# Forgetting attention and a two-layer MLP on one core: more of the first layer by seven products

## The chip, the core and the metric

The kernel runs on one core of one Trainium2 chip. The metric is the device time of one execution in microseconds (us); lower is better. A core has a matrix engine (TensorE, PE in the profile, with its weight loads as PEld), a vector engine (VectorE, DVE), a scalar engine for activations and copies (ScalarE, ACT), a general engine (GpSimd, POOL), and SyncE (SP), which here only issues DMAs. SBUF is the on-chip memory with 128 partitions; PSUM takes the results of PE.

## The reference, cut to what matters

```python
# attention: B=8, H=8, S=576, D=64, float32 in and out
scores = scale * q @ k.T                       # scale = 1/8
cum    = cumsum(log(clip(f, 1e-4, 1)), -1)     # f: [B, H, S]
scores = where(causal, -1e9, scores + cum[..., :, None] - cum[..., None, :])
attn   = exp(scores - max(scores)); attn = attn / (sum(attn) + 1e-9)
x      = (attn @ v).transpose(0, 2, 1, 3).reshape(4608, 512)
# MLP: w_in [512, 2048], w_out [2048, 512]
g      = gelu_tanh(x @ w_in)
out    = g @ w_out                             # [4608, 512] float32
```

## The kernel before

**Tiling.** The 64 heads are worked through in 16 quads of four (quad i = 0..15, batch i // 2). The MLP goes over the 4608 tokens in nine chunks of 512 (c = 0..8). Attention writes its output transposed into `xT`, 128 partitions by 4 blocks of features by 4608 tokens, in bf16. The MLP of a chunk starts when the quads that cover its tokens are done. A *stage* below is one chunk: its first layer, then its second layer mixed with the attention of quads that later chunks need.

**Order.** Nothing is scheduled by a planner. Each engine works through its instructions in the order in which they are written, and that order is written by hand as tables of short words: `SETUP`, `FRONT` (attention of the first quads, chunks 0 and 1) and `TABLES[2]` to `TABLES[8]`. `run` and `play` look up each word and issue its instructions. In a table, `q2` means quad 2c + 2, and numbers behind dots are arguments. What may overlap is set by semaphores between engines and by the number of buffers per pool: in PSUM two of `psS` (scores, and first-layer results), one of `psO` (attention products, and one first-layer block when asked for), two of `psM` (second layer and parts of the units); in SBUF four of `snap` and four of `ostage`.

**Words of the attention.** `LK`, `LQ` load keys and queries (issued on POOL's queue), `TK`, `TQ` transpose them (DVE, 1.24 us each), `S` computes scores (PE, L261) and their exponentials (ACT, L269), `M` masks with a select on POOL (L275), `m` masks by a product with a triangle on DVE (L304), `VW` or `vw` weights the values (POOL or DVE), `CL` copies a corner of them, `D` computes denominators (PE, then two transposes and a reciprocal on DVE, L348 to L352, `den`), `V` multiplies by the values on PE into `po` (L329) and then by the reciprocal on DVE into `xT` (L360), in two halves `V.i.0` and `V.i.1`. `LV` loads values from SP's queue. `Y` and `X` load the tables of gelu and of exp on ACT.

**Words of the first layer.** `P.pr` (`mlp_in`) computes 256 features of all 512 tokens: eight matmuls 128x512 (L374) and one gelu 128x1024 (L381); pr = 0..7. `P.pr.1` puts the result into `psO` instead of `psS`. `R.k` (`seven_in`) advances a *unit*: it replaces the two blocks pr = k and pr = k + 4 by Strassen's method with seven products instead of eight, on a 2 by 2 split of weights and tokens. It is a generator; each `R.k` in a table runs it to its next `yield`. One unit is 28 matmuls 128x256 (L422) in seven groups of four, into two banks of `psS` (pa, pb) and two of `psM` (pc, pd); on DVE one copy p1 (L435) and five additions that build p1, u2 and v4 in `snap` tiles (L437, L440, L442, L448, L452); four gelus 128x512 (L431). The unit needs sums of token blocks (`T`, four DVE operations at L395, kept in the columns of `xT` of the chunk before) and of weight blocks (`K.k.n`, n = 0..3, four DVE operations at L410). The first three sums of weights of unit k are kept in the columns of `xT` of chunk `HOMES[k]`, which are no longer needed; the fourth is made in place in `w_in_sb`.

**Words of the second layer.** `O`, `F` and `f` advance the second layer of a chunk by that many groups (`seven_products`, L510; also by seven products on a 2 by 2 split). It needs sums of the gelus, `G` (`gelu_sums`, DVE L489 to L495), copies two of its products out on ACT (L531) and adds on DVE into `o_st` (L535), which SP stores. `O.512` at the head of each table finishes the second layer of the chunk before; `F.10 S.q3.0 D.q2 ... f.22 ...` mixes the current one with attention.

Units before: chunk 3 has one (R.1), chunks 4 to 8 have two (R.1 and R.3), the others none. In table 7 the first layer is the line

```python
Y O.512 P.0.1 R.1 P.4.1 R.1 R.1 R.3 P.2.1 R.3 G.0.1.2 P.6 R.3 G.0.3.4 G.1.1.2 F.40 T
```

so a block `P` stands between two parts of a unit and gives DVE time to finish its additions.

Of the kernel before, what the change touches and what calls it, by code (L numbers as in the profile page):

```python
# [16 lines left out]
def kernel(  # L17
# [21 lines left out]
    N_DT = D_MODEL // 128  # L39
# [6 lines left out]
    CH = 512  # L46
# [31 lines left out]
        J.0.2 J.1.2 X LK.4 F.0.6 TK.3 B.3.256 S.2.0 LK.5 F.0.9 S.2.2 F.0.10 S.2.1 TQ.3 TQ.4 F.0.10 LV.2.0@LK.5 m.2.1 vw.2 TK.4 S.3.0 f.0.1 M.2.2  # L78
        CL.2 LQ.5 M.2.0 D.2 f.0.6 S.3.1 m.3.0 F.0.6 V.2.0 S.3.2 TK.5 LK.6 M.3.2 f.0.7 V.2.1 CL.3 S.4.1 m.3.1 LQ.6 F.0.6 TQ.5 H.4.2.1 D.3 H.4.0.1
        LQ.7 VW.4 H.4.0.0 V.3.1 v.3.0 f.0.3 H.4.2.0 CL.4 I.1.0 m.4.1 U.0 LV.2.1@LQ.5 I.1.4 TQ.6 m.4.2.3 I.1.1 I.1.5 U.1 LV.3.0@LQ.7 LV.3.1 m.4.2.2  # L80
        TK.6 G.0 M.4.0 LK.7 LQ.8 LK.8 I.1.2 I.1.3 U.3 I.1.6 I.1.7 G.1.1.2 U.2 X F.1.16 S.5.0 f.1.26 S.5.1 D.4 M.5.0 f.1.16 S.5.2 V.4.0 m.5.2.3
        f.1.10 VW.5 V.4.1 CL.5 m.5.2.2 S.6.0 f.1.10 M.5.1 D.5 f.1.7 S.6.1 V.5.1 f.1.12 V.5.0 vw.6 S.6.2 m.6.1 M.6.2.2 m.6.0 m.6.2.3 CL.6
    """

    HOMES = {1: 0, 3: 1}
    TABLES = {}
    TABLES[2] = """
        Y O.512 P.0 P.1 TK.q3 TQ.q3 LK.q5 LQ.q5 TK.q4 TQ.q4 LK.q6 LQ.q6 LV P.4 P.5 G.0 P.2 P.3 P.6 P.7 G.1.1.2 X F.10 S.q3.0 D.q2 M.q3.0 f.22 S.q3.1
        V.q2.0 K.1.0 K.1.1 M.q3.1 VW.q3 f.18 S.q3.2 V.q2.1 M.q3.2 K.3.0 K.3.1 CL.q3 f.16 S.q4.0 VW.q4 D.q3 M.q4.0 f.18 S.q4.1 V.q3.0 K.1.2 K.1.3 K.3.2
# [15 lines left out]
        M.q4.1 f.13 V.q3.1 T f.3 CL.q4 S.q4.2  # L105
    """
    TABLES[6] = """
        Y O.512 P.0.1 R.1 P.4.1 R.1 R.1 LK.q5 LQ.q5 M.q2.2 LV R.3 P.2.1 R.3 G.0.1.2 P.6 R.3 G.0.3.4 G.1.1.2 X F.10 S.q3.0 D.q2 M.q3.0 f.22 S.q3.1
        V.q2.0 M.q3.1 VW.q3 f.18 S.q3.2 V.q2.1 M.q3.2 CL.q3 f.20 D.q3 f.18 V.q3.0 v.q3.1 T f.14
    """  # L110
    TABLES[7] = """
        Y O.512 P.0.1 R.1 P.4.1 R.1 R.1 R.3 P.2.1 R.3 G.0.1.2 P.6 R.3 G.0.3.4 G.1.1.2 F.40 T
    """
    TABLES[8] = """
        O.512 P.0.1 R.1 P.4.1 R.1 R.1 R.3 P.2.1 R.3 G.0.1.2 P.6 R.3 G.0.3.4 G.1.1.2
    """

    singles = ctx.enter_context(tc.tile_pool(name="singles", bufs=1))
    ostage_pool = ctx.enter_context(tc.tile_pool(name="ostage", bufs=4))
    snap_pool = ctx.enter_context(tc.tile_pool(name="snap", bufs=4))  # L120
    den_pool = ctx.enter_context(tc.tile_pool(name="den", bufs=1))
    rb_pool = ctx.enter_context(tc.tile_pool(name="rb", bufs=2))
    psS = ctx.enter_context(tc.tile_pool(name="psS", bufs=2, space=bass.MemoryType.PSUM))
    psO = ctx.enter_context(tc.tile_pool(name="psO", bufs=1, space=bass.MemoryType.PSUM))
    psM = ctx.enter_context(tc.tile_pool(name="psM", bufs=2, space=bass.MemoryType.PSUM))

    def many(n, shape, dtype, name):
        return [singles.tile(shape, dtype, name=f"{name}{i}") for i in range(n)]

    ident_f32 = singles.tile([BH, BH], FP32, name="ident_f32")  # L130
    utri_f32 = singles.tile([128, 128], FP32, name="utri_f32")
    ones_f32 = singles.tile([128, 128], FP32, name="ones_f32")

    q_c = many(2, [128, S // 32, D], BF16, "q_c")
    k_c = many(2, [128, S // 32, D], BF16, "k_c")
# [227 lines left out]
    def mlp_in(c, prs, spare=0):  # L363
# [40 lines left out]

    def w_sums(k, eng, which):

        a11, a12, a21, a22, s1, s2, s4 = w_blocks(k)
        todo = ((s1, a21, a22), (s2, s1, a11), (s4, a12, s2), (a21, a11, a21))
        for n in which or range(4):
            (eng.tensor_sub if n else eng.tensor_add)(*todo[n])  # L410

    def seven_in(c, k):

        a11, a12, s3, a22, s1, s2, s4 = w_blocks(k)
        b11, b12, b21, b22, t1, t2, t3, t4 = x_blocks(c)
        pa, pb = (psS.tile([128, 2, 512], FP32, name="ps_ab", tag="s")[:, 0].rearrange("p (j n) -> p j n", j=2) for _ in range(2))
        pc, pd = (psM.tile([128, 2, HC], FP32, name="ps_cd", tag="m") for _ in range(2))

        def multiply(ps, w, x, first):
            for j in range(2):  # L420
                for dt in range(2):
                    nc.tensor.matmul(ps[:, j], w[:, dt, 128 * j:128 * j + 128], x[:, dt],  # L422
                                     start=(first and j == 0 and dt == 0), stop=(dt == 1),
                                     skip_group_check=True)
# [10 lines left out]
        nc.vector.tensor_copy(p1, pa)  # L435
        multiply(pb, s2, t2, True)
        nc.vector.tensor_add(u2, pb, p1)  # L437
        multiply(pc, s1, t1, True)
        v4 = part()
        nc.vector.tensor_add(v4, pc, u2)  # L440
        multiply(pd, s3, t3, True)
        nc.vector.tensor_add(v4, pd, v4)  # L442
# [12 lines left out]

# [209 lines left out]
    def load_values(b, half):  # L665
# [35 lines left out]
        "F": out_part,  # L701
        "f": lambda c, n: out_part(c, n, 1),
        "K": lambda k, *which: w_sums(k, nc.vector, which),
        "B": keep_busy,
        "X": load_exp,
        "Y": load_gelu,
# [81 lines left out]
```

## Time and profile before

| | us |
|---|---|
| median of three runs (lowest, highest) | 325.47 (325.46, 325.60) |
| the profiled execution | 325.69 |
| its span (first to last instruction) | 324.00 |
| PE busy, 5479 instructions | 312.9 (97%) |
| DVE busy, 381 instructions | 242.2 (75%) |
| ACT busy, 245 instructions | 202.8 (63%) |
| POOL busy, 150 instructions | 107.8 (33%) |
| first layer of chunk 2 (no unit) | 101.92 to 115.76: 13.84 |
| first layer of chunk 3 (one unit) | 136.39 to 149.81: 13.42 |
| first layer of chunk 7 (two units) | 269.48 to 282.64: 13.16 |

Times in rows of the profile are microseconds from the span's start unless they are called ns. A row of the timeline gives the start, the busy time, the engine, the line of the kernel, the operation, the output and input by the kernel's names, the shapes and types, and how many instructions in a run it joins. Matmuls are pipelined, so the busy time of a run of them is longer than the distance to the next; the pace is read from the starts. A bracket gives the idle time ahead of a row and who ended it. Some matmul records are missing (a row with x7 where eight were issued).

### The profile page before, as it was taken

What the parts mean: (1) busy time and instruction counts of PE and PEld (TensorE: products, weight loads), DVE (VectorE), ACT (ScalarE), POOL (GpSimd) and SP (SyncE); (2) the same over time, 40 slices, a digit from 0 to 9 for tenths busy, and PEclk for the clock granted to TensorE, in tenths of its full rate; (3) what the DMA queues carried; (4) which work ended last, traced back from release to release, by engine and by line L of the source; (5) the groups of instructions that cost most, each with busy time, mean ns of one, the idle gap of its engine ahead of it and who ended that gap; (6) DMA issues with size and microseconds to landing.
All of it is one profiled execution on the core that took longest, in us unless ns stands there. A gap on an engine that the chain in (4) does not pass through costs nothing.

```text
span 324.0 us, 12192 instructions
## 1 busy us (share of the span) xinstructions
PE 312.9 (97%) x5479; PEld 214.5 (66%) x5499; DVE 242.2 (75%) x381; ACT 202.8 (63%) x245; POOL 107.8 (33%) x150
## 2 busy tenths in 40 slices
PE   3999999999999999999999999999999999999995
PEld 1357854544776467766777687667866786687684
DVE  5676138895769748978996899789977967885772
ACT  4585586776767677577657785678666842722630
POOL 8987554340320217302662047303720140000000
PEclk9999999999999999999999999999999999999999
DMA  7999999779201951285129611981120102012003
GB/s 130 204 208 209 194 225 203 151 142 234 58 4 67 220 108 36 67 177 79 36 66 182 149 36 36 166 195 38 36 67 0 35 15 89 0 35 97 3 32 99
DMA packets 46485, 33.45 MB, mean 103 GB/s; under 512 B 29792, under 2 KB 40160, under 8 KB 46432
## 3 DMA queue, kind: packets, MB, share of 16 engines
q0 software_dynamic: 8624, 15.99, 28.4%
q1 hardware_dynamic: 37664, 16.60, 19.4%
q8 instruction: 43, 0.70, 1.0%
q14 instruction: 10, 0.08, 0.1%
q10 hardware_dynamic: 144, 0.07, 0.1%
HBM read 36.85 MB, written 9.44 MB: 143 GB/s over the span
## 4 chain that ended last, share of the span: by engine, by line
PE 94%; POOL 2%; issue 1%; ACT 1%; DVE 1%; POOLq 0%; DVEq 0%; ACTq 0%
PE ps_w L510 30%; PE ps_h L374 22%; PE ps_s L261 10%; PE po L329 9%; PE ps_cd L422 6%; PE ps_ab L422 5%; PE ps_h L464 4%; PE pso L580 4%; PE po_m L315 1%; PE idle_ps L240 1%; ACT pt L269 1%; POOL v_nat L169 1%; PE ps_o L329 0%; DVE pt L304 0%; POOL q_c L192 0%
## 5 line engine op out<-in xcount | busy, mean ns | idle before, releaser
L269 ACT ACTIVATE pt<-ps_s 128x1024 bf16<-128x1024 f32 (+2 forms) x100 | 93.7, 988 | 36.9 <-PE ps_s L261 32.5
L275 POOL TENSOR_SCALAR_AFFINE_SELECT pt<-pt 128x512 bf16<-128x512 bf16 (+3 forms) x65 | 39.0, 610 | 117.5 <-ACT pt L269 116.5
L374 PE MATMUL ps_h<-xT,w_in_sb 128*128 128x512 bf16 x320 | 75.7, 379 | 0.8
L381 ACT ACTIVATE gT<-ps_h 128x1024 bf16<-128x1024 f32 x42 | 42.9, 1021 | 40.5 <-PE ps_h L374 40.1
L374 PEld LDWEIGHTS <-w_in_sb 128*128 128x128 bf16 x336 | 32.8, 98 | 34.6 <-issue 0.4
L510 PEld LDWEIGHTS <-gT 128*32 128x32 bf16 (+1 forms) x1247 | 50.7, 97 | 5.7 <-issue 1.7
L510 PE MATMUL ps_w<-w_out_sb,gT 128*32 128x256 bf16 (+1 forms) x1050 | 46.9, 273 | 0.0
L510 PEld LDWEIGHTS <-gsum 128*32 128x32 bf16 (+1 forms) x1256 | 39.1, 97 | 1.4
L261 PE MATMUL ps_s<-qT,kT 32*128 32x64 bf16 (+5 forms) x896 | 36.6, 265 | 0.1
L510 PE MATMUL ps_w<-usum,gsum 128*32 128x256 bf16 (+1 forms) x832 | 30.6, 273 | 0.0
L215 POOL TENSOR_TENSOR vw<-v_nat,wT 128x1280 bf16<-128x1280 f32 (+1 forms) x13 | 30.5, 2346 | 0.1
L198 DVE STREAM_TRANSPOSE kT<-k_c 128x576 f32<-128x576 f32 x16 | 19.9, 1244 | 14.1 <-DMA k_c<-in_k_dram 14.1
L535 DVE TENSOR_TENSOR o_st<-ps_w,snap 128x512 f32<-128x512 f32 x31 | 21.3, 690 | 10.5 <-PE ps_w L510 8.7
L261 PEld LDWEIGHTS <-kT 32*128 32x128 bf16 x896 | 16.6, 93 | 17.2 <-issue 12.3
L360 DVE TENSOR_TENSOR xT<-po,rb 128x576 bf16<-128x576 f32 x26 | 19.5, 751 | 5.9 <-PE po L329 5.4
L329 PE MATMUL po<-pt,vw 128*32 128x64 bf16 (+4 forms) x624 | 22.5, 279 | 0.0
L329 PEld LDWEIGHTS <-vw 128*32 128x32 bf16 x672 | 14.2, 97 | 10.5 <-issue 3.7
L422 PEld LDWEIGHTS <-w_in_sb 128*128 128x128 bf16 x176 | 17.2, 98 | 5.1 <-issue 0.8
L198 DVE STREAM_TRANSPOSE qT<-q_c 128x576 f32<-128x576 f32 x16 | 19.9, 1244 | 0.9 <-PE ps_s L261 0.7
L431 ACT ACTIVATE gT<-snap 128x512 bf16<-128x512 f32 x33 | 18.8, 623 | 0.7
L489 DVE TENSOR_TENSOR gsum<-gT 128x1024 bf16<-128x1024 bf16 x16 | 11.0, 685 | 11.1 <-ACT gT L381 11.1
L510 PE MATMUL ps_w<-usum,gT 128*128 128x256 bf16 (+1 forms) x197 | 16.9, 273 | 0.0
(100 smaller groups left out, 420.4 us busy)
## 6 DMA issues: line engine op xcount, KB each, us to landing
out_dram<-o_st SPq DMA_DIRECT2D x35, 256.0 KB, 2.3
k_c<-in_k_dram POOLq DMA_DIRECT2D x16, 288.0 KB, 5.5
q_c<-in_q_dram POOLq DMA_DIRECT2D x16, 288.0 KB, 6.9
v_nat<-in_v_dram SPq DMA_DIRECT2D x16, 256.0 KB, 6.1
v_nat<-in_v_dram SPq DMA_DIRECT2D x20, 128.0 KB, 4.9
w_in_sb<-in_moe_w_in_dram POOLq DMA_DIRECT2D x4, 512.0 KB, 10.0
w_out_sb<-in_moe_w_out_dram POOLq DMA_DIRECT2D x4, 512.0 KB, 8.8
v_nat<-in_v_dram POOLq DMA_DIRECT2D x9, 128.0 KB, 6.8
```

What stands on the lines that cost most here:

```text
L198: nc.vector.transpose(out=dst.rearrange("p s c -> p (s c)").bitcast(FP32) .rearrange("p (t a) -> p a t", a=S // 32), in_=src.rearrange("p ...
L215: eng.tensor_mul(vw[i % 2][:, t0:t1], vb[:, t0:t1, h0:h0 + 4, :], wT[:, i, t0:t1, :].unsqueeze(3).to_broadcast([128, t1 - t0, 4, D]))
L261: nc.tensor.matmul(tiles[h // 2][:, h % 2, c0:c0 + nq], key_columns(i, key, h, c), qq[32 * h:32 * h + 32, q0:q0 + nq, c], start=(c == 0 an ...
L269: nc.scalar.activation(p[:, 2 * g:2 * g + 2, off:off + n], t[:, :, 0:n], AF.Exp, scale=scale)
L275: nc.gpsimd.affine_select(out=x, in_=x, compare_op=ALU.is_ge, fill=0.0, base=0, pattern=pattern, channel_multiplier=-1)
L329: nc.tensor.matmul(po[r0:r0 + w.shape[-1], 448 + q0:448 + q0 + nq], w, p[:, h, col:col + nq], start=(key in (0, "low")), stop=(key in ("lo ...
L360: nc.vector.tensor_mul(xT[:, 2 * u + x, S * b + s0:S * b + s1], po, rbs[i, part])
L374: nc.tensor.matmul(ph[:, j, :], w_in_sb[:, dt, 128 * ft:128 * ft + 128], xT[:, dt, CH * c:CH * (c + 1)], start=(dt == 0), stop=(dt == N_DT ...
L381: nc.scalar.activation(gT[:, 2 * pr:2 * pr + 2, :], ph, AF.Gelu_apprx_tanh)
L422: nc.tensor.matmul(ps[:, j], w[:, dt, 128 * j:128 * j + 128], x[:, dt], start=(first and j == 0 and dt == 0), stop=(dt == 1), skip_group_c ...
L510: nc.tensor.matmul(ps[c0:c0 + width, n, cols[0]:cols[1]], x[:, j, 128 * n + c0:128 * n + c0 + width], w[:, j, cols[0]:cols[1]], start=(fir ...
L535: nc.vector.tensor_add(st, ps, kept[name])
```

## The change

Four more units. Chunk 2 gets R.1, chunk 3 gets R.3 as well, and chunks 7 and 8 get a third one, R.0. Chunks 4 to 6 keep two. With that:

- In `FRONT` the weight sums K.1 and the token sums of chunk 2 (`T.2`, a new word there) are made. The masks of quad 6 and CL.6 move from the end of `FRONT` into table 2.
- Table 2 takes the order that table 3 had, plus those masks and K.3; its loads LK.q6, LQ.q6 move to the head of table 3. Table 3 takes the order of table 4.
- Table 6 makes the weight sums of unit 0: K.0.0 to K.0.2 ahead of `G.1.1.2`, K.0.3 at the end. They lie in the columns of chunk 2.
- In tables 7 and 8 a unit is started by `R.k.1`. Then p1 is copied by ACT instead of DVE, there are more yields, and the gelu of p1 comes after the last phase. The two blocks that are left (pr = 2 and 6) are computed in halves, `p`, of four matmuls each in `psO`, between phases of the units.
- `snap` gets six buffers for four. Four setup tiles are moved into tiles that are used later only.

```diff
-        TK.6 G.0 M.4.0 LK.7 LQ.8 LK.8 I.1.2 I.1.3 U.3 I.1.6 I.1.7 G.1.1.2 U.2 X F.1.16 S.5.0 f.1.26 S.5.1 D.4 M.5.0 f.1.16 S.5.2 V.4.0 m.5.2.3
-        f.1.10 VW.5 V.4.1 CL.5 m.5.2.2 S.6.0 f.1.10 M.5.1 D.5 f.1.7 S.6.1 V.5.1 f.1.12 V.5.0 vw.6 S.6.2 m.6.1 M.6.2.2 m.6.0 m.6.2.3 CL.6
+        TK.6 G.0 M.4.0 LK.7 LQ.8 LK.8 I.1.2 I.1.3 U.3 K.1.0 K.1.1 K.1.2 I.1.6 I.1.7 G.1.1.2 U.2 X F.1.16 S.5.0 f.1.26 S.5.1 D.4 M.5.0 f.1.16 S.5.2
+        V.4.0 m.5.2.3 f.1.10 VW.5 V.4.1 K.1.3 CL.5 m.5.2.2 S.6.0 f.1.10 M.5.1 D.5 f.1.7 S.6.1 V.5.1 f.1.12 V.5.0 T.2 S.6.2 vw.6
     """
-    HOMES = {1: 0, 3: 1}
+    HOMES = {1: 0, 3: 1, 0: 2}
     TABLES[2] = """
-        Y O.512 P.0 P.1 TK.q3 TQ.q3 LK.q5 LQ.q5 TK.q4 TQ.q4 LK.q6 LQ.q6 LV P.4 P.5 G.0 P.2 P.3 P.6 P.7 G.1.1.2 X F.10 S.q3.0 D.q2 M.q3.0 f.22 S.q3.1
-        V.q2.0 K.1.0 K.1.1 M.q3.1 VW.q3 f.18 S.q3.2 V.q2.1 M.q3.2 K.3.0 K.3.1 CL.q3 f.16 S.q4.0 VW.q4 D.q3 M.q4.0 f.18 S.q4.1 V.q3.0 K.1.2 K.1.3 K.3.2
-        M.q4.1 f.9 V.q3.1 f.7 T CL.q4 S.q4.2
+        Y O.512 P.0.1 R.1 P.4.1 R.1 R.1 TK.q3 TQ.q3 LK.q5 LQ.q5 m.q2.1 M.q2.2.2 m.q2.0 m.q2.2.3 CL.q2 LV P.2 G.0 P.3 K.3.0 K.3.1 K.3.2 P.6 P.7 K.3.3
+        G.1.1.2 X F.10 S.q3.0 D.q2 M.q3.0 f.22 S.q3.1 V.q2.0 TK.q4 TQ.q4 M.q3.1 VW.q3 f.18 S.q3.2 V.q2.1 M.q3.2 TK.q5 CL.q3 f.16 S.q4.0 VW.q4 D.q3
+        M.q4.0 f.18 S.q4.1 TQ.q5 V.q3.0 M.q4.1 f.13 V.q3.1 T f.3 CL.q4 S.q4.2
     """
     TABLES[3] = """
-        Y O.512 P.0.1 R.1 P.4.1 R.1 R.1 TK.q3 TQ.q3 LK.q5 LQ.q5 M.q2.2 LV P.2 G.0 P.3 P.6 P.7 G.1.1.2 X F.10 S.q3.0 D.q2 M.q3.0 f.22 S.q3.1 V.q2.0
-        K.3.3 TK.q4 TQ.q4 M.q3.1 VW.q3 f.18 S.q3.2 V.q2.1 M.q3.2 TK.q5 CL.q3 f.16 S.q4.0 VW.q4 D.q3 M.q4.0 f.18 S.q4.1 TQ.q5 V.q3.0 M.q4.1 f.13
-        V.q3.1 T f.3 CL.q4 S.q4.2
+        Y O.512 LK.q4 LQ.q4 P.0.1 R.1 P.4.1 R.1 R.1 LK.q5 LQ.q5 M.q2.2 LV R.3 P.2.1 R.3 G.0.1.2 P.6 R.3 G.0.3.4 G.1.1.2 X F.10 S.q3.0 D.q2 M.q3.0
+        f.22 S.q3.1 V.q2.0 TK.q4 TQ.q4 M.q3.1 VW.q3 f.18 S.q3.2 V.q2.1 M.q3.2 TK.q5 CL.q3 f.16 S.q4.0 VW.q4 D.q3 M.q4.0 f.18 S.q4.1 TQ.q5 V.q3.0
+        M.q4.1 f.13 V.q3.1 T f.3 CL.q4 S.q4.2
     """
     TABLES[6] = """
-        Y O.512 P.0.1 R.1 P.4.1 R.1 R.1 LK.q5 LQ.q5 M.q2.2 LV R.3 P.2.1 R.3 G.0.1.2 P.6 R.3 G.0.3.4 G.1.1.2 X F.10 S.q3.0 D.q2 M.q3.0 f.22 S.q3.1
-        V.q2.0 M.q3.1 VW.q3 f.18 S.q3.2 V.q2.1 M.q3.2 CL.q3 f.20 D.q3 f.18 V.q3.0 v.q3.1 T f.14
+        Y O.512 P.0.1 R.1 P.4.1 R.1 R.1 LK.q5 LQ.q5 M.q2.2 LV R.3 P.2.1 R.3 G.0.1.2 P.6 R.3 G.0.3.4 K.0.0 K.0.1 K.0.2 G.1.1.2 X F.10 S.q3.0 D.q2
+        M.q3.0 f.22 S.q3.1 V.q2.0 M.q3.1 VW.q3 f.18 S.q3.2 V.q2.1 M.q3.2 CL.q3 f.20 D.q3 f.18 V.q3.0 v.q3.1 T f.14 K.0.3
     """
     TABLES[7] = """
-        Y O.512 P.0.1 R.1 P.4.1 R.1 R.1 R.3 P.2.1 R.3 G.0.1.2 P.6 R.3 G.0.3.4 G.1.1.2 F.40 T
+        Y O.512 R.1.1 R.1 p.2 R.1 R.1 R.0.1 R.1 R.0 p.2 R.0 R.0 R.3.1 R.0 R.3 p.6 R.3 R.3 p.6 R.3 G.0.1.2 G.1.1.2 G.0.3.4 F.40 T
     """
     TABLES[8] = """
-        O.512 P.0.1 R.1 P.4.1 R.1 R.1 R.3 P.2.1 R.3 G.0.1.2 P.6 R.3 G.0.3.4 G.1.1.2
+        O.512 R.1.1 R.1 p.2 R.1 R.1 R.0.1 R.1 R.0 p.2 R.0 R.0 R.3.1 R.0 R.3 p.6 R.3 R.3 p.6 R.3 G.0.1.2 G.1.1.2 G.0.3.4
     """
...
-    snap_pool = ctx.enter_context(tc.tile_pool(name="snap", bufs=4))
+    snap_pool = ctx.enter_context(tc.tile_pool(name="snap", bufs=6))
...
+    gates = g4.rearrange("p t n -> p (t n)").bitcast(FP32)
+    logfT, before, ones_f32 = gates[:, 0:NT * BH], gates[:, NT * BH:(2 * NT - 1) * BH], gates[:, 1024 - 128:1024]
+    idle = u4.rearrange("p t n -> p (t n)")[:, 0:512]
...
+    def mlp_in_halves(c, pr):
+
+        ph = psO.tile([128, 1024], FP32, name="ps_h", tag="po").rearrange("p (a n) -> p a n", a=2)
+        for j in range(2):
+            for dt in range(N_DT):
+                nc.tensor.matmul(ph[:, j, :], w_in_sb[:, dt, 128 * (2 * pr + j):128 * (2 * pr + j) + 128],
+                                 xT[:, dt, CH * c:CH * (c + 1)], start=(dt == 0), stop=(dt == N_DT - 1))
+            if j:
+                nc.scalar.activation(gT[:, 2 * pr:2 * pr + 2, :], ph, AF.Gelu_apprx_tanh)
+            yield
...
-    def seven_in(c, k):
+    def seven_in(c, k, act=0):
...
-        p1, u2 = part(), part()
-        nc.vector.tensor_copy(p1, pa)
+        p1, u2, v4 = part(), part(), part()
+        if act:
+            nc.scalar.copy(p1, pa)
+            yield
+        else:
+            nc.vector.tensor_copy(p1, pa)
         multiply(pb, s2, t2, True)
         nc.vector.tensor_add(u2, pb, p1)
         multiply(pc, s1, t1, True)
-        v4 = part()
         nc.vector.tensor_add(v4, pc, u2)
...
         nc.vector.tensor_add(p1, pc, u2)
-        gelu(0, 1, p1)
+        if not act:
+            gelu(0, 1, p1)
         yield
         multiply(pd, a22, t4, False)
         nc.vector.tensor_add(u2, pd, u2)
+        if act:
+            yield
+            gelu(0, 1, p1)
         gelu(1, 0, u2)
         yield
```

More of the change, by code (lines that the diff above doesn't have):

```diff
@@ L131 @@
     utri_f32 = singles.tile([128, 128], FP32, name="utri_f32")
-    ones_f32 = singles.tile([128, 128], FP32, name="ones_f32")
     q_c = many(2, [128, S // 32, D], BF16, "q_c")
@@ L149 @@
     f_sb = g2.rearrange("p t n -> p (t n)").bitcast(FP32)[0:BH, 0:S]
-    logfT = singles.tile([128, NT * BH], FP32, name="logfT")
-    before = singles.tile([128, (NT - 1) * BH], FP32, name="before")
     wT = singles.tile([128, NQ, NT, 4], FP32, name="wT")
@@ L154 @@
     shift = singles.tile([128, 1], FP32, name="shift")
-    idle = singles.tile([128, 512], BF16, name="idle")
+    gates = g4.rearrange("p t n -> p (t n)").bitcast(FP32)
+    logfT, before, ones_f32 = gates[:, 0:NT * BH], gates[:, NT * BH:(2 * NT - 1) * BH], gates[:, 1024 - 128:1024]
+    idle = u4.rearrange("p t n -> p (t n)")[:, 0:512]
     spare = singles.tile([1, 1], FP32, name="spare")
@@ L703 @@
         "K": lambda k, *which: w_sums(k, nc.vector, which),
+        "T": lambda c, *which: x_sums(c, which or range(4), nc.vector),
         "B": keep_busy,
@@ L718, in run @@
             dmas[word.replace("LP", "LU").replace("LX", "LV")] = did[-1]
-    units = {}
-    def seven(c, k):
-        next(units.setdefault((c, k), seven_in(c, k)))
+    units, halves = {}, {}
     def quads(call):
@@ L734 @@
         "P": lambda c, pr, spare=0: mlp_in(c, (pr,), spare),
-        "R": lambda c, k: next(units.setdefault((c, k), seven_in(c, k))),
+        "R": lambda c, k, *how: next(units.setdefault((c, k), seven_in(c, k, *how))),
+        "p": lambda c, pr: next(halves.setdefault((c, pr), mlp_in_halves(c, pr))),
         "TT": lambda c, *which: x_sums(c, which or range(4), nc.vector),
```

## The prediction

> **What bounds the kernel now.** I read the busy shares first, then the chain that ended last, then the order of PE and DVE through the first layer. Busy shares, granted clock and chain, from the page:
>
> ```profile
> PE 312.9 (97%) x5479; PEld 214.5 (66%) x5499; DVE 242.2 (75%) x381; ACT 202.8 (63%) x245; POOL 107.8 (33%) x150
> ...
> PEclk9999999999999999999999999999999999999999
> ...
> PE 94%; POOL 2%; issue 1%; ACT 1%; DVE 1%; POOLq 0%; DVEq 0%; ACTq 0%
> ```
>
> PE holds 94% of the chain at full clock: fewer PE columns shorten the run, unless another engine comes late. DVE at 75% is next. PE in chunk 7's first layer (start, us, engine, line, operation):
>
> ```profile
> 269.48 1.89 PE L374 MATMUL ps_h<-xT,w_in_sb 128*128 128x512 bf16 x7
> 271.20 0.60 PE L422 MATMUL ps_ab<-xT,w_in_sb 128*128 128x256 bf16 x4
> 271.64 0.60 PE L422 MATMUL ps_ab<-xT 128*128 128x256 bf16 x4
> ...
> 273.38 1.89 PE L374 MATMUL ps_h<-xT,w_in_sb 128*128 128x512 bf16 x8
> 275.11 0.60 PE L422 MATMUL ps_cd<-xT 128*128 128x256 bf16 x4
> ...
> 277.29 0.60 PE L422 MATMUL ps_cd<-xT,w_in_sb 128*128 128x256 bf16 x4
> 277.88 0.60 PE L422 MATMUL ps_ab<-xT,w_in_sb 128*128 128x256 bf16 x4
> ...
> 282.64 1.58 PE L510 MATMUL ps_w<-w_out_sb,gT 128*128 128x256 bf16 x13
> ```
>
> Starts give the pace. Eight 128x512 matmuls go by in 275.11 − 273.38 = 1.73 us (0.2163 each), four 128x256 in 271.64 − 271.20 = 0.437 (0.1092 each). A unit is 28 small ones, 3.06 us; the two blocks it replaces are 16 large ones, 3.46. So a unit saves 0.40 us of PE. Only one gap is there: 277.29 to 277.88 is 0.59 where 0.44 is due, 0.15 lost. DVE at that place:
>
> ```profile
> 277.15 0.68 DVE L435 COPY snap<-ps_ab 128x512 f32<-128x512 f32 x1
> 277.96 0.69 DVE L437 TENSOR_TENSOR snap<-ps_ab,snap 128x512 f32<-128x512 f32 x1
> 278.79 0.69 DVE L440 TENSOR_TENSOR snap<-ps_cd,snap 128x512 f32<-128x512 f32 x1
> 279.58 0.69 DVE L442 TENSOR_TENSOR snap<-ps_cd,snap 128x512 f32<-128x512 f32 x1
> ```
>
> The fifth product reuses the bank that the copy reads, and the copy ends at 277.83. Dependent DVE steps follow at 0.80 us, independent ones at 0.60 (275.75, 276.54, 277.15 in the same view).
>
> **The change, part by part.** The profiled run took 325.69 us for its span of 324.00, so 1.69 lies around the span; the median of the runs, 325.47, is 0.22 below the profiled run. I sum changes of the span and take them off the median.
>
> *Chunk 2, no unit to one.* The stage takes the form that chunk 3 had. First layer: chunk 2 runs 101.92 to 115.76 (13.84), chunk 3 136.39 to 149.81 (13.42): −0.42, the unit's 0.40. The rest of the stage: 115.76 to 136.39 (20.63) against 149.81 to 170.40 (20.59): −0.04, and S.q3.0 to S.q3.0 (116.92, 151.00, 184.76) gives periods of 34.08 and 33.76. I take −0.47. Its cover is DVE. DVE was busy 26.33 us of 34.47 in chunk 2. Added: six adds and copies of the unit at 0.69 (4.1), x sums now before the layer (1.7, with the old ones for chunk 3 still at its end), one more pair of transposes (2 × 1.24), less three weight sums at about 0.65: some +6.2 net, 32.5 of 34.0. Walked through instruction by instruction: the x sums run 100.5–102.2, vw.6 (1.48) to 103.6, o_st to 104.2 (the fourth product's bank waits for it, wanted at 104.96), unit to 108.2, TK.7/TQ.7 to 111.7, the masks moved from FRONT to 112.7, CL.6 (0.22), G.0 to 115.7, K.3.0–3 to 117.3, G.1.1.2 to 118.6, den 118.5–119.3 where V.6.0 wants its PSUM at about 121.0, and level at 120.6. No PE stall, 1.7 us spare. The loads LK/LQ of the quad after next stand on POOL's queue behind TK.7/TQ.7 (110.7, 111.8), M.6.2.2 behind them, done by about 113.5: D.6 reads that mask at 117.6, and a load lands in 5.5 to 6.9 us (by 119), for transposes after V.6.1 (124). SP's order is kept. Bounds: 0 to +0.8 of stall for POOL beside DVE's bf16 operations (rows under c).
>
> *Chunk 3, one unit to two.* It becomes chunk 4's stage, word for word: 13.42 to 13.18 (the unit's 0.40 less the 0.15 gap) and the rest 20.59 to 20.51, −0.08. **−0.32.** K.3 is ready a stage earlier.
>
> *FRONT.* K.1.0–2 (L410 took 0.42 alone, up to 0.85 beside POOL) fall in DVE's idle 3.03 us ahead of 82.66 and cost nothing. K.1.3 (0.42, in place at 0.35 pace) lies ahead of CL.5 and m.5.2.2, which ended at 95.03; D.5's matmuls on that key start about 95.22. So D.5 is late by 0.35 + 0.04 − 0.19 ≈ 0.2: bounds 0.07 to 0.25, **+0.18**. The copies of ones, logfT, before and idle into other tiles keep order and waits: 0. Snap's six buffers: 0.
>
> *Chunk 6.* K.0.0–2 push DVE's next work by 3 × 0.41 = 1.235: G.1.1 from 252.96 to 254.19. den is then free at 256.34 (V.q2.0 wants 256.52), o_st ends 257.33 + 0.6, G.1.3 and G.1.4 end 259.1, xT 259.14–259.89 where V.q2.1 wants 259.85: **+0.08**. These rows of before show the place and what threatens it (DVE, then POOL):
>
> ```profile
> 257.53 0.68 DVE L495 TENSOR_TENSOR gsum<-gT,gsum 128x1024 bf16<-128x1024 bf16 x1
> 258.13 0.75 DVE L360 TENSOR_TENSOR xT<-po,rb 128x576 bf16<-128x576 f32 x1
> 260.77 0.76 DVE L360 TENSOR_TENSOR xT<-po,rb 128x576 bf16<-128x576 f32 x1 [1.90 <-PE po L329]
> ```
>
> ```profile
> 258.75 0.64 POOL L275 TENSOR_SCALAR_AFFINE_SELECT pt<-pt 128x512 bf16<-128x512 bf16 x1 [1.73 <-ACT pt L269]
> ```
>
> G.1.4 would start at 258.54, 0.2 us ahead of POOL's select at 258.75. If the select comes first, G.1.4 can wait for its 0.64 us: bounds 0 and +0.75.
> The Trainium skill (SBUF — State Buffer, "Who interferes with whom") says that a DVE instruction with two SBUF inputs contends with a GpSimd instruction that reads SBUF, and that whoever issues first blocks the other. The slow rows under c agree; by that rule 258.54 against 258.75 decides, 0 or 0.65.
>
> *Chunk 7, two units to three.* PE work falls by 0.40; the 0.15 gap goes, since p1 is copied by ACT (nearest row: L531, same shape, 0.576 against DVE's 0.686) and a half block stands ahead of the second phase. New waits: K.0.3 at the end of chunk 6 delays o_st p7 to 270.17–270.86, and pd, wanted at 270.78, gets its bank at 270.90: 0.12. In each unit the last product reuses pd, which v4's second add must have read: from the unit's start p1 is copied by 1.26, then u2 (1.30), v4 (2.10), v4 again (2.89 to 3.54 with semaphore), against five small groups, a half block and one small group on PE, 2.18 + 0.87 + 0.44 = 3.49: about 0.03 to 0.09 a unit, 0.03 + 0.09 + 0.08 here. End 282.43 for 282.64: **−0.21**.
>
> *Chunk 8.* The same without K.0.3: 0.10 + 0.09 + 0.08 of waits, **−0.27**. Behind it the second layer runs with less cover: its j=6 gelu ready 310.07 (wanted 310.18), G.1.2 310.96 (wanted 311.27), o_st 312.81 (wanted 313.02). All just make it. Bounds for 7 and 8: −0.55 each with no waits, +0.5 each when all three margins break.
>
> Sum: −0.47 − 0.32 + 0.18 + 0.08 − 0.21 − 0.27 = −1.01, span 322.99, the profiled run 324.68, **median 324.46 us**. Best case, no new wait at all: −0.47 − 0.32 − 0.55 − 0.55 = −1.89, 323.6. Worst by the bounds: +0.8 + 0.75 + 1.0 over the forecast, about 327.
>
> **The rivals.**
> (a) The forecast, 324.46: PE keeps its cover, four units save.
> (b) DVE becomes the bound in chunks 7 and 8. For it: DVE was busy 9.8 of 13.2 us in that layer, and each third unit adds four or five operations of 0.6 to 0.8 in 12.6 us; every phase is a chain of dependent steps 0.80 apart. Against: the half blocks give each chain 0.87 us more. If each of six units waited 0.15 to 0.25 us, the last two chunks would give nothing and the rest −0.5 remains: 325.0 to 325.5, within the noise.
> (c) The other side, slower: DVE's bf16 sums are held up by POOL in chunk 2. DVE (first two rows) beside POOL (third) in before:
>
> ```profile
> 86.51 0.93 DVE L493 TENSOR_TENSOR gT<-gT 128x1024 bf16<-128x1024 bf16 x1
> 87.36 1.14 DVE L495 TENSOR_TENSOR gsum<-gT,gsum 128x1024 bf16<-128x1024 bf16 x1
> ```
>
> ```profile
> 86.50 1.47 POOL L275 TENSOR_SCALAR_AFFINE_SELECT pt<-pt 64x256 bf16<-64x256 bf16 x2 [11.88 <-ACT pt L269]
> ```
>
> Usually 0.68 each; a third, L493 at 146.95, took 2.07 beside a load's issue and two selects, 1.39 more. With 32.5 of 34.0 us busy and 1.7 spare, three such operations (4.2) make PE 2.5 late: 324.46 + 2.5 = 327.0. It becomes slower by 0.2% once more than 1.7 + 1.7 = 3.4 us are held. Against: only the two loads, M.6.2.2 and three selects lie there.
> (d) Units save nothing: if the large matmul went by at well under twice the small one's pace, 28 for 16 would cost. In this trace the ratio is 0.2163 to 0.1092, so 1.75 × 0.505 = 0.88. At equal pace for both, four units would add 4 × 12 × 0.109 = 5.2 us: about 330.7.
> The Trainium skill (TensorE: Matmul & The Clock Gate, "Back-to-back issue gap") gives 131 ns for 512 columns and 81 for 128 in a sustained stream with weight loads; by it a unit would cost 2.3 us or more against 2.1. The trace's 216 ns contradicts it.
>
> **How the numbers follow.** (a) 0.63, (b) 0.21, (c) 0.15, (d) 0.01. (b) lies wholly inside 0.2% of the median (0.65 us, 324.82 to 326.12, about what a measurement can tell); (c) and (d) are slower. Faster 0.63, same 0.21, slower 0.16. The range takes (a) with its best case and (b): 323.7 to 325.6, leaving (c), (d) out; (a) alone 323.7 to 324.9.
>
> **What would show it.** Right: first layers of 13.4 us in chunk 2, 13.2 in chunk 3 and 12.9 in chunks 7 and 8; no idle PE before D or V of chunks 2 and 6 over 0.1 us; periods between S.q3.0 of chunks 2 to 4 equal to 33.7 to 33.8. Wrong: DVE rows over 0.9 us beside POOL in 100 to 121 us; PE gaps of over 0.1 at each unit's last product; a PE wait ahead of the second layer's third or fourth product in the last stage; K.1.3's stall over 0.3.

## The result: 0.4% slower, lost in chunk 2

The changed kernel takes 326.73 us (median of six runs, 326.42 to 326.90) against 325.47 before: a ratio of 1.004, 95% interval 1.0027 to 1.0053. The forecast was 324.46 with 323.7 to 325.6; the sign was wrong. The profiled run has a span of 325.1 us for 324.0.

Busy shares, granted clock and the chain that ended last, from the page of the changed kernel (its lines are numbered otherwise: L374 is L373 there, L422 is L432, L510 is L527, L535 is L552):

```profile
PE 312.4 (96%) x5527; PEld 219.0 (67%) x5547; DVE 255.9 (79%) x407; ACT 206.8 (64%) x259; POOL 107.3 (33%) x150
...
PEclk9999999999999999999999999999999999999999
...
PE 87%; DVE 7%; POOL 2%; issue 2%; ACT 1%; POOLq 0%; DVEq 0%; ACTq 0%
```

PE fell from 94% to 87% of the chain and DVE rose from 1% to 7%: PE waited for DVE somewhere. The starts of the first layers, read from the order of PE in both kernels, say where (us; a stage runs from the start of its first layer to the next; chunk 8 of the kernel before starts at 294.87, its first matmul is missing from the trace; the first layer of its chunk 2 ends at 115.73, so it takes 13.81 and not 13.84):

| | before | forecast of the change | after | change |
|---|---|---|---|---|
| start of chunk 2 | 101.92 | +0.18 | 101.92 | 0.00 |
| stage of chunk 2 (first layer) | 34.47 (13.81) | −0.47 | 36.05 (13.42) | +1.58 |
| stage of chunk 3 (first layer) | 34.01 (13.42) | −0.32 | 33.68 (13.17) | −0.33 |
| stages of chunks 4 and 5 | 33.69, 33.69 | 0 | 33.68, 33.68 | −0.02 |
| stage of chunk 6 | 31.70 | +0.08 | 31.78 | +0.08 |
| stage of chunk 7 (first layer) | 25.39 (13.16) | −0.21 | 25.30 (13.07) | −0.09 |
| first layer of chunk 8 | 13.18 | −0.27 | 13.10 | −0.08 |
| from there to the end | 15.95 | 0 | 15.91 | −0.04 |

Chunk 2 is 2.05 us worse than forecast; chunks 7 and 8 give 0.31 less than forecast; all else is within 0.2. PE's waits, summed over the changed kernel (engine, line, what was waited for: us, times, longest), have two rows for attention that the kernel before does not have:

```profile
PE ps_w L527 <- DVE o_st L552: 0.9, 1, 0.9
PE po L328 <- DVE xT L359: 0.7, 1, 0.7
```

On the timeline of PE they lie in the second half of chunk 2:

```profile
128.18 1.70 PE L527 MATMUL ps_w<-w_out_sb,gT 128*32 128x256 bf16 x56
130.82 0.62 PE L527 MATMUL ps_w<-w_out_sb,gsum 128*32 128x256 bf16 x16 [0.94 <-DVE o_st L552]
...
132.63 1.49 PE L527 MATMUL ps_w<-w_out_sb,gsum 128*32 128x256 bf16 x48
133.94 0.28 PE L527 MATMUL ps_w<-usum,gT 128*32 128x256 bf16 x4
134.95 0.87 PE L328 MATMUL po<-pt,vw 128*32 128x512 bf16 x24 [0.73 <-DVE xT L359]
```

The first of these stretches in the kernel before:

```profile
128.58 1.70 PE L510 MATMUL ps_w<-w_out_sb,gT 128*32 128x256 bf16 x56
130.11 0.61 PE L510 MATMUL ps_w<-w_out_sb,gsum 128*32 128x256 bf16 x16
```

From start to start the first stretch takes 2.64 us where the kernel before took 1.53, the second 1.01 where 0.11 is due (as in the experiment with the copy on ScalarE, below): 1.11 + 0.90 = 2.01 us, nearly all of the 2.05 by which chunk 2 missed. DVE, and then POOL, ahead of the first wait:

```profile
126.71 1.24 DVE L197 STREAM_TRANSPOSE kT<-k_c 128x576 f32<-128x576 f32 x1
127.98 2.07 DVE L219 COPY vw<-vw 64x256 bf16<-64x256 bf16 x1
130.08 0.69 DVE L552 TENSOR_TENSOR o_st<-ps_w,snap 128x512 f32<-128x512 f32 x1
```

```profile
127.64 2.33 POOL L214 TENSOR_TENSOR vw<-v_nat,wT 128x1280 bf16<-128x1280 f32 x1
```

A copy of 64x256 elements, 0.22 us alone, takes 2.07 us. It starts 0.34 us after POOL's weighting of the next quad's values and ends 0.08 us after it. In the kernel before, the same copy at the same place of chunk 3 was 0.18 us ahead of POOL (DVE, then POOL):

```profile
161.99 0.28 DVE L220 COPY vw<-vw 64x256 bf16<-64x256 bf16 x1
```

```profile
162.17 2.33 POOL L215 TENSOR_TENSOR vw<-v_nat,wT 128x1280 bf16<-128x1280 f32 x1
```

### The profile page after: what moved, and what is told of

Read it like the earlier page. It is cut to its first block, busy times and chain, and to the rows that moved or that the text cites. A ratio compares the mean times of both kernels' runs of the same rounds, so it can differ in the third digit from the quotient of the medians.

```text
span 325.1 us, 12342 instructions
## 1 busy us (share of the span) xinstructions
PE 312.4 (96%) x5527; PEld 219.0 (67%) x5547; DVE 255.9 (79%) x407; ACT 206.8 (64%) x259; POOL 107.3 (33%) x150
## 4 chain that ended last, share of the span: by engine, by line
PE 87%; DVE 7%; POOL 2%; issue 2%; ACT 1%; POOLq 0%; DVEq 0%; ACTq 0%
PE ps_w L527 27%; PE ps_h L373 14%; PE ps_s L260 9%; PE po L328 9%; PE ps_cd L432 8%; PE ps_ab L432 6%; PE ps_h L481 4%; PE pso L597 4%; PE ps_h L387 2%; PE po_m L314 1%; PE idle_ps L239 1%; DVE pt L303 1%; ACT pt L268 1%; POOL v_nat L168 1%; DVE kT L197 1%
## 5 line engine op out<-in xcount | busy, mean ns | idle before, releaser
L373 PE MATMUL ps_h<-xT,w_in_sb 128*128 128x512 bf16 x228 | 54.5, 379 | 0.6
L527 PEld LDWEIGHTS <-gT 128*32 128x32 bf16 (+1 forms) x1247 | 50.6, 97 | 6.0 <-issue 1.7
L527 PE MATMUL ps_w<-w_out_sb,gT 128*32 128x256 bf16 (+1 forms) x1050 | 46.9, 273 | 0.0
L380 ACT ACTIVATE gT<-ps_h 128x1024 bf16<-128x1024 f32 x30 | 30.6, 1020 | 17.2 <-PE ps_h L373 16.7
L527 PEld LDWEIGHTS <-gsum 128*32 128x32 bf16 (+1 forms) x1256 | 39.2, 97 | 2.5 <-issue 1.1
L373 PEld LDWEIGHTS <-w_in_sb 128*128 128x128 bf16 x240 | 23.4, 98 | 24.3 <-issue 0.4
L527 PE MATMUL ps_w<-usum,gsum 128*32 128x256 bf16 (+1 forms) x832 | 30.6, 273 | 0.0
L441 ACT ACTIVATE gT<-snap 128x512 bf16<-128x512 f32 x45 | 26.1, 625 | 3.0 <-DVE snap L455 2.4
L432 PEld LDWEIGHTS <-w_in_sb 128*128 128x128 bf16 x240 | 23.4, 98 | 6.2 <-issue 1.5
L552 DVE TENSOR_TENSOR o_st<-ps_w,snap 128x512 f32<-128x512 f32 x31 | 21.3, 687 | 7.5 <-PE ps_w L527 6.1
L432 PEld LDWEIGHTS <-xT 128*128 128x128 bf16 x180 | 17.6, 98 | 5.2
L191 POOL DMA_DIRECT2D k_c<-in_k_dram x16 | 9.2, 576 | 27.8 <-DVE kT L197 22.4
```

What stands on the lines that cost most here:

```text
L373: nc.tensor.matmul(ph[:, j, :], w_in_sb[:, dt, 128 * ft:128 * ft + 128], xT[:, dt, CH * c:CH * (c + 1)], start=(dt == 0), stop=(dt == N_DT ...
L527: nc.tensor.matmul(ps[c0:c0 + width, n, cols[0]:cols[1]], x[:, j, 128 * n + c0:128 * n + c0 + width], w[:, j, cols[0]:cols[1]], start=(fir ...
L552: nc.vector.tensor_add(st, ps, kept[name])
```

## The experiments

Theory 1: the copy `CL.7` is held by POOL's product `VW.8`, and the rest of the loss follows from it. No data ties the two: `CL.7` stands ahead of `VW.8` in the program and works in the other of the two `vw` tiles. Theory 2: DVE, busy for 33.75 of the stage's 36.05 us (1.85 of them the copy beyond its usual 0.22), simply has too much to do.

**The held copy, taken away in two ways.** First the copy alone goes to ScalarE:

```diff
-  ... V.q2.1 M.q3.2 TK.q5 CL.q3 f.16 S.q4.0 VW.q4 D.q3      (table 2)
+  ... V.q2.1 M.q3.2 TK.q5 cl.q3 f.16 S.q4.0 VW.q4 D.q3
+  "cl": lambda i: nc.scalar.copy(vw[i % 2][64:128, LOW], vw[i % 2][0:64, 0]),
```

> The changed kernel, with the corner copy of quad 7's values in chunk 2 (the DVE row of 64x256 that took 2.07 us, 127.98 to 130.05, beside POOL's 128x1280 product of 127.64 to 129.97) made on ScalarE. Theory 1, the held copy: PE's waits of 0.94 us for o_st (130.82) and 0.73 us for xT (134.95) both come from it; without it o_st starts about 128.0 and both waits go: chunk 2 takes about 34.4 us for 36.05, the median is about 325.1 us. Theory 2, DVE has simply too much to do in chunk 2 (it was 0.8 to 1.0 us behind my walk by 121.4): taking away a copy that normally lasts 0.22 us gives no more than that and the 0.4 us by which the copy was late: 326.1 us or more, with the PE wait for xT still there.

Then nothing is taken from DVE, and POOL's product moves instead:

```diff
-  ... TK.q5 CL.q3 f.16 S.q4.0 VW.q4 D.q3 M.q4.0 f.18      (table 2)
+  ... TK.q5 CL.q3 f.16 S.q4.0 D.q3 M.q4.0 VW.q4 f.18
```

> The changed kernel, with POOL's 128x1280 product of quad 8's values moved behind the next two selects in chunk 2, so that the corner copy stays on DVE in its place but has no POOL work beside it. Theory 1, the held copy: the copy takes 0.22 to 0.43 us, both PE waits go, about 325.1 us, like the copy on ScalarE. Theory 2, too much work on DVE: DVE has exactly the same work, so 326.7 us is kept within 0.2.

Beside 325.50 before: 325.04 us with the copy on ScalarE (0.9975, interval 0.9949 to 1.0001) and 324.96 with the product later (0.9983, 0.9950 to 1.0017). Both intervals lie below that of the changed kernel, 1.0027 to 1.0053; neither is clearly below the kernel before. Chunk 2 takes 34.00 and 34.20 us for 36.05, and neither wait of PE is left over 0.2 us. In the second run DVE has all its work, and the copy runs as usual:

```profile
128.07 0.22 DVE L219 COPY vw<-vw 64x256 bf16<-64x256 bf16 x1
128.33 0.69 DVE L552 TENSOR_TENSOR o_st<-ps_w,snap 128x512 f32<-128x512 f32 x1
```

So DVE's load alone costs PE no more than 0.2 us in chunk 2 once the copy is not held; theory 2, as the cause of the loss, falls.

**The same loss, made in the kernel before.** Two memsets of an unused tile delay DVE ahead of the copy of chunk 4:

```diff
-  ... M.q3.2 TK.q5 CL.q3 f.16 S.q4.0 VW.q4 ...      (table 4 of the kernel before)
+  ... M.q3.2 TK.q5 DL CL.q3 f.16 S.q4.0 VW.q4 ...
+  "DL": lambda c: [nc.vector.memset(idle, 0.0) for _ in range(2)],
```

> The kernel before, with two memsets of an unused 128x512 bf16 tile on DVE (0.27 us each in the setup) ahead of the corner copy in chunk 4, where that copy starts at 195.53, 0.32 us ahead of POOL's 128x1280 product at 195.85. Nothing else is added. Theory 1: the copy comes after POOL's start and is held until about 198.2, o_st ends 1.9 to 2.3 us later than 196.7, PE waits about 0.9 to 1.0 us for it and perhaps 0.5 for xT: +0.9 to +1.7 us on the span, 326.4 to 327.2 us. Theory 2: DVE is only 0.55 us later, o_st ends 197.2 and PE wants that bank at 197.87: no wait for it, 325.5 us.

It takes 327.44 us against 325.50 (1.0052, 1.0027 to 1.0078); the stage of chunk 4 takes 35.78 us for 33.69. DVE, POOL and PE there:

```profile
194.81 0.66 DVE L743 MEMSET idle<- 128x256 uint32 x2
195.50 2.09 DVE L220 COPY vw<-vw 64x256 bf16<-64x256 bf16 x1
197.62 0.69 DVE L535 TENSOR_TENSOR o_st<-ps_w,snap 128x512 f32<-128x512 f32 x1
```

```profile
195.18 2.33 POOL L215 TENSOR_TENSOR vw<-v_nat,wT 128x1280 bf16<-128x1280 f32 x1
```

```profile
198.37 0.62 PE L510 MATMUL ps_w<-w_out_sb,gsum 128*32 128x256 bf16 x16 [1.00 <-DVE o_st L535]
...
202.50 0.86 PE L329 MATMUL po<-pt,vw 128*32 128x512 bf16 x24 [0.73 <-DVE xT L360]
```

0.66 us of DVE work cost 2.09 us of time, with the same two waits of PE as in the changed kernel. The delay put the copy behind POOL's start; the rest is the held copy. My upper bound of +1.7 was too low by 0.4, because I had added up brackets of idle time, and they do not show all that PE loses (in the changed kernel 2.01 us from start to start, 1.67 in the brackets).

**Chunks 6 to 8 alone.** Tables 6, 7 and 8 of the change, with `FRONT` and tables 2 and 3 as before:

```diff
-  FRONT, TABLES[2], TABLES[3] of the changed kernel
+  FRONT, TABLES[2], TABLES[3] of the kernel before
```

> Only the part of the change in chunks 6 to 8: FRONT and tables 2 and 3 as in the kernel before. From the traces of both kernels: chunk 6 +0.09 us, chunk 7 -0.09, chunk 8 -0.08 and -0.04 behind it, -0.1 in all: 325.35 us, no measurable change. If the last product of each unit did not wait (0.16 us, six times, less the first, where it was 0.02), it would be -0.9. If instead the parts act on each other (chunk 2 late makes 7 and 8 late), the last chunks alone would give the -0.40 that I forecast for them: 325.1.

325.29 us (0.9993, 0.9959 to 1.0026): no change that can be measured. The first layers take 13.07 and 13.10 us, as in the changed kernel, so the small gain in chunks 7 and 8 is their own and does not hang on chunk 2. PE and DVE in one unit of chunk 8 of the changed kernel:

```profile
303.21 0.60 PE L432 MATMUL ps_cd<-xT 128*128 128x256 bf16 x4
303.81 0.60 PE L432 MATMUL ps_cd<-xT,w_in_sb 128*128 128x256 bf16 x4
```

```profile
301.47 0.69 DVE L451 TENSOR_TENSOR snap<-ps_ab,snap 128x512 f32<-128x512 f32 x1 [0.22 <-ACT snap L446]
302.27 0.69 DVE L453 TENSOR_TENSOR snap<-ps_cd,snap 128x512 f32<-128x512 f32 x1
303.06 0.69 DVE L455 TENSOR_TENSOR snap<-ps_cd,snap 128x512 f32<-128x512 f32 x1
```

The last product starts 0.60 us after the one ahead of it, where 0.44 is due: 0.16 lost. It adds to the bank that v4's second addition reads, which ends at 303.06 + 0.69 = 303.75, 0.06 us ahead of the product's start. Five of the six units lose 0.16 in this way, the first one 0.02.

**What sets that wait.** On the base of the copy on ScalarE, p1 of each unit in chunks 7 and 8 goes back to DVE:

```diff
-            nc.scalar.copy(p1, pa)
+            nc.vector.tensor_copy(p1, pa)
```

> The changed kernel with the corner copy of chunk 2 on ScalarE (325.0 us), and in chunks 7 and 8 the copy p1 of each unit back on DVE; the order of words stays. It tells what the copy on ScalarE is worth. Theory a, DVE's chain of dependent additions sets the pace of three units in a row (five steps of 0.795 us a unit, 4.0, against 3.9 us of PE): a sixth step a unit makes 4.6 to 4.8 us, so each chunk gets 0.7 to 0.8 us longer, the first layers take about 13.8 us for 13.1, the median is about 326.5. Theory b, the waits of 0.16 us come from ScalarE's copy being late: they get shorter, 325.0 or less.

326.95 us against 325.55 (1.0043, 1.0020 to 1.0065). The first layers take 14.52 and 14.04 us for 13.29 and 13.10 of the base: the direction of theory a, and more than its 0.7 to 0.8 (1.23 and 0.94). PE now waits ahead of each of the last two products of a unit, 0.30 and 0.36 us in the first of chunk 7. Theory b, by which the waits would get shorter, falls.

In the other direction, work goes between the product and the addition that it waits for:

```diff
-  R.1.1 R.1 p.2 R.1 R.1 R.0.1 R.1 R.0 p.2 R.0 R.0 R.3.1 R.0 R.3 p.6 R.3 R.3 p.6 R.3 G.0.1.2 G.1.1.2 G.0.3.4
+  R.1.1 R.1 p.2 R.1 R.0.1 R.1 R.1 R.0 p.2 R.0 R.3.1 R.0 R.0 R.3 p.6 R.3 p.6 G.0.1.2 R.3 R.3 G.1.1.2 G.0.3.4
...
-        pc, pd = (psM.tile(...) for _ in range(2))      (seven_in, ahead of the unit's first product)
+        pc, pd = (psM.tile(...) for _ in range(2))      (seven_in, behind the copy p1)
```

> The same base (325.0 us); in chunks 7 and 8 the first product of the next unit is put ahead of the last product of the current one, the second half block ahead of the third unit's last product, and the first gelu sums ahead of that product too. No work is added or taken away. Theory a: the last product waits 0.16 us because v4's second addition ends 3.64 us after the unit's start and PE is there at 3.49; with 0.44 us of other work between, the waits go to 0.07 or nothing, the first layers take about 12.75 us for 13.1: 324.3 us. Theory b (ScalarE is the late one): the next unit's copy comes no earlier, waits move to the next unit's second product, no gain: 325.0.

324.39 us (0.9969, 0.9940 to 0.9997). The base's interval, 0.9949 to 1.0001, overlaps this one, so this gain and the next are read from the first layers and not from the medians. Chunk 8's first layer takes 12.76 us for 13.10, as expected; chunk 7's takes 13.14 for 13.29.

**The fourth weight sums.**

```diff
-  ... V.4.1 K.1.3 CL.5 m.5.2.2 S.6.0 ...      (FRONT)
+  ... V.4.1 CL.5 m.5.2.2 K.1.3 S.6.0 ...
-  ... CL.q3 f.20 D.q3 f.18 V.q3.0 v.q3.1 T f.14 K.0.3      (table 6)
+  ... CL.q3 f.20 K.0.3 D.q3 f.18 V.q3.0 v.q3.1 T f.14
```

> The same base (325.0 us); the fourth weight sum of unit 1 moves behind the masks of quad 5 in the first part, that of unit 0 from the end of chunk 6 to DVE's idle time ahead of the denominators of the last quad. If the 0.17 us of PE wait at the denominators of quad 5 (95.48) and the 0.11 us at the unit's fourth product in chunk 7 (272.22) are what these two sums cost, both go and the median is 324.75; if the wait in chunk 7 is due to the token sums ahead, not to this sum, only 0.17 goes.

324.90 us (0.9973, 0.9952 to 0.9995), expected 324.75, and by the medians not to be told from the base. The stretch of PE at D.5 is back to 0.68 us (0.85 in the changed kernel), and the wait ahead of chunk 7's fourth product is gone (0.44 from start to start for 0.55). But that layer takes 13.21 us for 13.29, a gain of only 0.08.

**All of them, and a miss.** The copy on ScalarE, the new order and the moved sums together:

> All three together on the changed kernel: corner copy on ScalarE, the next unit's first product first, fourth sums moved. If the gains are independent, 326.73 - 1.7 - 0.7 - 0.28 = 324.05 us, 0.44% below the kernel before; if all of them draw on the same slack of DVE, no better than 324.5.

324.20 us (0.9951, 0.9929 to 0.9974), expected 324.05. By the stages each gain stands beside the others: chunk 2 takes 34.01, the first layers of chunks 7 and 8 take 13.03 and 12.75. Then the same with POOL's product moved instead of the copy:

> As the version with all three changes (324.2 us), but the corner copy of chunk 2 is kept clear of POOL by moving POOL's 128x1280 product back instead of by a copy on ScalarE. Chunk 2 takes 34.2 us this way for 34.0, so +0.2. But in every run with the copy on ScalarE one DVE step of chunk 7's first unit came 0.35 us late and its first layer took 0.1 to 0.2 us longer than in the changed kernel, in the one run with the product moved it did not: if that belongs to the extra ScalarE instruction, chunk 7 takes 12.8 us for 13.03. Together 324.2, within 0.2.

324.17 us (0.9960, 0.9932 to 0.9988), the same. Chunk 2 takes 34.20 for 34.01, chunk 7's layer 12.76 for 13.03, both as expected. Then every unit of chunks 3 to 6 with its copy on ScalarE too:

```diff
-  P.0.1 R.1 P.4.1 R.1 R.1 LK.q5 LQ.q5 M.q2.2 LV R.3 P.2.1 R.3 G.0.1.2 P.6 R.3 G.0.3.4      (tables 3 to 6)
+  P.0.1 R.1.1 R.1 P.4.1 R.1 R.1 LK.q5 LQ.q5 M.q2.2 LV R.3.1 R.1 R.3 P.2.1 R.3 G.0.1.2 P.6 R.3 R.3 G.0.3.4
```

> The same, and in chunks 3 to 6 both units also take their copy p1 on ScalarE, with the second unit's first product ahead of the first unit's last gelus. It tests the other half of the reading of the gap in these chunks (PE waits 0.15 us in each, because the first product's bank is read by a DVE copy that stands behind the first unit's last addition): if that is its cause, the four first layers take 13.03 us for 13.17 and the median falls by 0.5 to 0.6, to about 323.6. If the gap comes from something else, nothing changes.

325.12 us (0.9987, 0.9961 to 1.0013): 0.95 slower than without it, where 0.55 faster was expected, and the stages of chunks 3 to 6 are longer by 0.27, 0.27, 0.26 and 0.19 us. The 0.15 us gap of the second unit was gone, but the first unit had a new one, PE first, then ACT:

```profile
138.53 0.60 PE L431 MATMUL ps_cd<-xT,w_in_sb 128*128 128x256 bf16 x4
139.20 0.60 PE L431 MATMUL ps_ab<-xT,w_in_sb 128*128 128x256 bf16 x4
```

```profile
136.28 1.28 ACT L232 ACT_TABLE_LOAD   x1
...
137.68 1.00 ACT L380 ACTIVATE gT<-ps_h 128x1024 bf16<-128x1024 f32 x1
138.59 0.56 ACT L445 COPY snap<-ps_ab 128x512 f32<-128x512 f32 x1
```

The copy stands behind the table load and the first gelu and ends at 139.15: PE loses 0.23. Behind the layer the first exponential was later as well, and chunks 3 to 5 lost another 0.19 us there, with a PE wait at the next scores. So only the second unit's copy went to ScalarE, with its own gelus in their old place:

```diff
-  P.0.1 R.1 P.4.1 R.1 R.1 ... LV R.3 P.2.1 R.3 G.0.1.2 P.6 R.3 G.0.3.4      (tables 3 to 6)
+  P.0.1 R.1.2 P.4.1 R.1 R.1 ... LV R.3.1 R.1 R.3 P.2.1 R.3 G.0.1.2 P.6 R.3 G.0.3.4
...
-        if act:
+        if act & 1:
             nc.scalar.copy(p1, pa)
             yield
...
-        if not act:
+        if not act & 2:
             gelu(0, 1, p1)
...
-        if act:
+        if act & 2:
             yield
             gelu(0, 1, p1)
```

> As the run before the last (324.17 us), and in chunks 3 to 6 only the second unit's copy p1 is made on ScalarE, with that unit's first product ahead of the first unit's last two gelus; the first unit's copy stays on DVE and the second unit's gelu of p1 stays ahead of the last block. Reading of the run with all copies on ScalarE (325.12): the 0.15 us gap of the second unit went, but the first unit's copy stood behind ScalarE's table load and the first gelu (PE waited 0.23 us), and two gelus after the last block put the first exponential off (PE waited 0.19 us at the next scores). If that is right, both new waits go, the four first layers take 13.03 us for 13.17, the rest of each chunk 20.5 as before, and the median is 0.5 to 0.6 lower, about 323.6. If the second unit's gap was not due to the DVE copy, 13.17 and 324.2 stay.

323.48 us against 325.64 (0.9929, 0.9912 to 0.9946): the four first layers take 13.02 us, those of chunks 7 and 8 12.76. The median is 0.69 us lower where 0.5 to 0.6 was expected; the four stages give 0.61. Against the kernel before this version is 0.7% faster.

## Why the prediction was wrong, step by step

**The step that failed is chunk 2: "level at 120.6. No PE stall, 1.7 us spare".** PE lost 2.01 us there, where the bound for work held by POOL was 0 to +0.8. Two things were wrong. First, the walk was short. It had the three masks moved from FRONT end at 112.7, with 1.0 us for the three; they ended at 113.70:

```profile
111.77 1.93 DVE L303 TENSOR_TENSOR pt<-pt,causal 128x512 bf16<-128x512 bf16 x3
```

Two of them took 0.40 and 0.41 us, the third 1.27, beside a load's issue and the select M.6.2.2 on POOL (112.76 to 113.41). At the end of FRONT in the kernel before, the same three took 1.52 us:

```profile
101.90 1.52 DVE L304 TENSOR_TENSOR pt<-pt,causal 128x512 bf16<-128x512 bf16 x3
```

There the third took 0.85, beside a select too. In both kernels the slow mask ends 0.27 to 0.29 us after the select does (113.70 and 113.41, 103.42 and 103.15). That POOL held it is argued from these times; no run takes the select away. So 1.0 was the price of masks alone, and a row of the kernel before had a higher one. ("Unit to 108.2" is a slip without effect: the unit ended at 109.68, and the 111.7 behind it allows for that.) The delay went on: o_st came at 121.44 for 120.60, and by the copy DVE was still 0.44 us behind the old chunk 3 (the row xT at 126.04, against 160.07 less 34.47).

Second, the slack was taken at the wrong place. 1.7 us is what V.6.0 could spare; the least slack of the stage was the 0.18 us by which the corner copy was ahead of POOL's product in the kernel before, a pair that the prediction never mentions. 0.44 us of delay against 0.18 of slack turned a copy of 0.22 us into one of 2.07.

**Rival (c) had the mechanism, DVE held up by POOL, with other operations and a wrong point of decision.** It asked for three held sums and 3.4 us. What was slow was one mask, by 0.86 us, and one copy, by 1.85; the copy was enough, since o_st, the next denominators and xT stand behind it in DVE's order with less slack than V.6.0. That the time of (c), 327.0, lies near 326.73 is luck. Its sign, a DVE row over 0.9 us beside POOL in 100 to 121 us, came true with the mask, but the copy at 127.98 lies behind the stretch that it watched. It got 0.15; with the rows of 1.52 and of 0.18 in view it should have had more.

The Trainium skill (SBUF — State Buffer, "Who interferes with whom") says that a copy can run in a two-port mode, that such a mode takes the port pair that DVE shares with GpSimd, that whoever issues first holds the pair for its whole instruction, and that a DVE instruction with at most one SBUF input outside those modes does not contend. The runs agree as to the order: the copy 0.32 us behind POOL's start took 2.09 us in the memset run, 0.18 us ahead of it 0.28; an addition with one input in SBUF and one in PSUM took its usual 0.69 us beside such a product (o_st at 128.51 beside POOL from 128.38, kernel before). Which mode the copy ran in, no run shows.

**Chunks 7 and 8: right mechanism, a term too small.** The wait of the last product for v4's second addition was put at 0.03 to 0.10 us a unit; it measured 0.16 in five of six. The bank is free 3.65 us after the unit's start, not 3.54 (in the rows above 303.81, in a unit that starts at 300.16): I let the addition free it after 0.61 us, DVE's pace, where its whole 0.69 counts. So −0.21 and −0.27 became −0.09 and −0.08. The wait for o_st, 0.12, measured 0.11. For the second layer behind, "All just make it" held: −0.04 us to the end.

**Right:** the unit saves 0.39 us of PE (13.81 to 13.42 in chunk 2, for 0.40), chunk 3 −0.33 for −0.32, chunk 6 +0.08 for +0.08 (POOL's select was held instead, 0.94 us for 0.64, as G.1.4 came first), K.1.3 +0.17 at D.5 for +0.18, which chunk 1's first layer, 0.16 us earlier in this run (67.36 for 67.52), cancelled. Rival (b) was right about chunks 7 and 8: DVE's chain does bound their units, and the waits of 0.16 us in five of six units lie in the 0.15 to 0.25 that it asked for; they leave 0.17 us of gain where it had none. Rival (d) is out: in chunk 2's first layer the pace of both matmul shapes gave the saving.

**Left open:** in the runs with the corner copy on ScalarE, one DVE step of chunk 7's first unit or two came 0.2 to 0.35 us late; with POOL's product moved it did not. The step is the unit's last addition. With the new order of words it starts 0.91 us after the product that it reads has started (324.39 and 324.20 us), and 0.64 in the run with POOL's product moved (324.17); the next group of products has gone by in the meantime. What ties this to the corner copy is not settled.

## What to carry to other kernels

Before adding work to an engine, list the pairs of operations on DVE and POOL whose order is decided by time alone, with their margins: there a delay of a few tenths is not passed on as it is but can cost the whole of the other engine's operation, as the copy beside the product did. Price an operation by the row in which the same neighbour ran beside it, not by the row in which it ran alone. Slack belongs to a place, not to a stage: take the smallest one that stands behind the added work, copies and small moves included. In a chain of dependent additions the last step frees its bank only after its full duration; other products between the chain and what waits for it took that wait away here (13.10 to 12.76 us in chunk 8).

## What the runs showed that I had not expected

A 64x256 bf16 copy between two places of SBUF waits out a 2.33 us product of POOL: 2.07 and 2.09 us in two kernels. Elsewhere in the kernel before and in the changed one it takes 0.22 to 0.54, and 0.70 in chunk 6 of the run with POOL's product later, where it starts 0.01 us behind a select (261.52 and 261.51). And 0.66 us of idle work on DVE, which is idle 25% of the time on average in that kernel, made the whole kernel about 1.9 us slower (327.44 for 325.50).
